# A gated scan and two feed-forward layers on one core: conversion of the weights on VectorE in pairs, the tanh ahead of the last block's cast, first tokens turned on TensorE

## The chip, the cores and the metric

The kernel runs on one core of one Trainium2 chip. The metric is the device time of an execution in microseconds (us); the time before is 2100.8 us, the median of three runs (2100.55 to 2101.74).

Engines are named as in the profile: PE is TensorE, DVE VectorE, ACT ScalarE, POOL GpSimd, SP the engine that issues most DMAs. Each executes its instructions in the order in which the program gives them, and waits where an operand isn't there yet.

## What is computed

```python
# x, f_logit: (2, 6080, 256)   weights: (256, 2048) and (2048, 256), 64-bit floats
f = lower_bound + (1 - lower_bound) / (1 + exp(-f_logit))
h = f[:, t] * h + (1 - f[:, t]) * x[:, t]      # for t in 6080 steps; y[:, t] = h
x = y.reshape(12160, 256)
h = x @ moe_w_in;   x = (h - tanh(h)) @ moe_w_out
h = x @ moe2_w_in;  return max(0.01 * h, h) @ moe2_w_out
```

The weights come as 64-bit floats, and the kernel reads them as pairs of 32-bit words. It multiplies with more precision than one product of TensorE's 32-bit format gives: each operand is split into a high half (rounded) and a low half (the rest), and three products are added up: high by high, high by low, low by high.

## The kernel before

The 12160 tokens are cut into macros of 1024 tokens. An item is one macro in one layer; items alternate between the layers. An item goes through 8 units of 256 hidden features. In the first three items (`NPLAIN`; layer 1, layer 1, layer 2) a unit is four **plain blocks** of 128 features by 512 tokens, 96 blocks in all; block s is the s-th. From the fourth item on a unit saves products with Strassen's scheme, in another loop.

A plain block is, in the loop over `order` at the end: `plain` (6 products into one of four PSUM banks, L381), `act` (the tanh, L391, or in layer 2 the leaky function, L393, on ACT), `shrink` (h - tanh(h), L399 on DVE, layer 1 only), then for its two halves `hi` (a rounding cast, L404 on ACT) and `lo` (the subtraction, L409 on DVE), and three blocks later `emit_B` (6 products with the output weights, L425). `rest` holds `hi` and `lo` of a block back until the products of the next one have been issued. `work(s)` runs what `put` has laid beside block s: conversion of weights, loads, the front end of the next macro and the splitting of its tokens (`make_forms`, `split_hi`, `split_lo`). All of it goes into the same engine queues, in the order of the code.

`convert` turns 256 columns of weights (one unit of w_in or w_out, 128 by 512 pairs of words) into high and low halves: L109, L115, L117, L127, L133 on DVE, L111, L121, L122 and the cast L135 on ACT, the addition L126 and the product L138 on POOL. The result goes to the tile that the unit uses (layer 1) or through a staging tile (layer 2), and to DRAM, from which later items stream it (`stream_a`, `stream_b`). Layer 1's units are converted during item 0, just ahead of their use, layer 2's during item 1. `sums_in` makes the four sums of blocks that Strassen's scheme needs, for a unit at a time.

The front end of a macro (`front`) turns f_logit and x so that features lie on the partitions: `load_tokens` reads runs of 32 features, and DVE transposes 32 by 32 blocks (L278). Then come the gate's tanh on ACT (L285), a scaling (L289), the input product (L296), and the scan in pieces of 256 tokens (L307).

Of the kernel before, what the change touches and what calls it, by code (L numbers as in the profile page):

```python
# [6 lines left out]

# [7 lines left out]
P = 128  # L15
# [4 lines left out]
def tile_gated_scan_two_ffn(  # L20
# [51 lines left out]

    lb = const.tile([P, KD], F32, name="lb")
# [19 lines left out]
    E_LO, E_HI = float(896 << 20), float(1151 << 20)  # L93

    def convert(load, halves, store):

        s = {}
        sh = [P, 2, 2 * P]

        def words(i, dt):  # L100
            return s["raw"].bitcast(dt).rearrange("p a (n t) -> p a n t", t=2)[:, :, :, i]

        def f0():
            s["raw"] = cv.tile(sh, U64, tag="raw", bufs=3, name="raw")
            nc.sync.dma_start(s["raw"], load)

        def s0():
            b = s["b"] = cv.tile(sh, I32, tag="b", bufs=2, name="b")
            nc.vector.tensor_scalar(b, words(1, I32), 0x7FFFFE00, None, op0=ALU.bitwise_and)  # L109
            s["l"] = cv.tile(sh, F32, tag="l", bufs=2, name="l")  # L110
            nc.scalar.activation(s["l"], words(0, U32), AF.Copy, scale=2.0**-52)  # L111

        def s1():
            b = s["b"]
            nc.vector.tensor_scalar(b, b, E_LO, E_HI, op0=ALU.max, op1=ALU.min)  # L115
            s["m"] = cv.tile(sh, I32, tag="m", bufs=2, name="m")
            nc.vector.tensor_scalar(s["m"], words(1, I32), 0x1FF, None, op0=ALU.bitwise_and)  # L117

        def s2():
            b = s["b"]  # L120
            nc.scalar.activation(b, b, AF.Copy, scale=8.0, bias=-8.0 * E_LO)  # L121
            nc.scalar.activation(s["m"].bitcast(F32), s["m"], AF.Copy, scale=2.0**-20)  # L122

        def s3():
            b = s["b"]
# [5 lines left out]
        def s4():  # L131
            s["e"] = cv.tile(sh, I32, tag="m", bufs=2, name="e")
            nc.vector.tensor_scalar(s["e"], s["b"], -(1 << 23), None, op0=ALU.bitwise_and)  # L133
            s["w"] = halves()
            nc.scalar.copy(s["w"][0], s["b"].bitcast(F32))  # L135

        def s5():
            nc.gpsimd.tensor_tensor(s["w"][1], s["l"], s["e"].bitcast(F32), ALU.mult)  # L138

        def s6():  # L140
            store()
            s.clear()

        return f0, [s0, s1, s2, s3, s4, s5, s6]

    def conv_in(l, u, dst):
# [13 lines left out]
        return convert(src, halves, store)  # L160

    def conv_out(l, u, dst):
# [10 lines left out]
        return convert(src, halves, store)  # L173

    def sums_in(l, u):

        s = {}
        sh = [P, 2, 2 * P]

        def v(i):  # L180
            return s["f"][:, i]

        def f0():
            s["raw"] = cv.tile(sh, U64, tag="raw", bufs=3, name="raw").bitcast(F32).rearrange(
                "p a (b q) -> p a b q", q=P
            )
            nc.sync.dma_start(s["raw"], wa_d[l][u][:, :, 0:4])

        def s0():
            s["f"] = cv.tile(sh, I32, tag="b", bufs=2, name="f").bitcast(F32).rearrange(  # L190
                "p k (f q) -> p (k f) q", q=P
            )
            nc.vector.tensor_tensor(s["f"], s["raw"][:, 0], s["raw"][:, 1], ALU.add)
            s["s"] = cv.tile(sh, F32, tag="l", bufs=2, name="s").rearrange(
                "p k (f q) -> p (k f) q", q=P
            )

        def s1():
            r = s["s"]
            nc.vector.tensor_tensor(r[:, 0], v(0), v(2), ALU.add)  # L200
            nc.vector.tensor_tensor(r[:, 2], v(1), v(0), ALU.subtract)

        def s2():
            r = s["s"]
            nc.vector.tensor_tensor(r[:, 1], r[:, 0], v(1), ALU.subtract)
            nc.vector.tensor_tensor(r[:, 3], v(3), r[:, 1], ALU.subtract)

        def s3():
            s["w"] = cv.tile([P, 2, 4, P], F32R, tag="sa", name="sa")
            nc.scalar.copy(s["w"][:, 0], s["s"])  # L210

        def s4():
            nc.vector.tensor_tensor(s["w"][:, 1], s["s"], s["w"][:, 0].bitcast(F32), ALU.subtract)

        def s5():
            nc.sync.dma_start(wa_d[l][u][:, :, 4:8], s["w"].bitcast(F32))
            s.clear()

        return f0, [s0, s1, s2, s3, s4, s5]
# [11 lines left out]

    def stage_a():
        return cv.tile([P, 2, 4, P], F32R, tag="sa", name="sa")

    def stage_b():
        return cv.tile([P, 2, 2, DM], F32R, tag="sb", name="sb")
# [18 lines left out]
    def load_tokens(c, k, nm, part=None, eng=None):  # L255

        t0, n = macros[c]
        a, e = part or (0, n)
        if (c, k, nm) not in raw:
            raw[c, k, nm] = fp.tile([P, 2 * H // 32, 32], F32, tag="raw", bufs=4, name=f"raw{nm}")  # L260
# [443 lines left out]
```

## Time and profile before

| | |
|---|---|
| median of three runs | 2100.8 us |
| the profiled execution | 2104.0 us |
| its span | 2102.2 us |
| TensorE busy | 2010.3 us, 96% of the span |
| VectorE busy | 1441.0 us, 69% |
| ScalarE busy | 1239.7 us, 59% |
| GpSimd busy | 85.8 us, 4%, all of it in the first 305 us |

The span is the part of the profiled execution between its first and last recorded instruction. Shares of the whole span hide stages: the plain blocks end at 380 us, a fifth of the way, and conversion lies within them. "Idle before" is the time for which an engine did nothing ahead of an instruction, with what released it. Where a row covers several instructions, its duration is that of all of them, from the first start to the last end; a start-to-start distance of two rows is what an instruction costs its engine in a dense stretch.

### The profile page before, as it was taken

What the parts mean: (1) busy time and instruction counts of PE and PEld (TensorE: products, weight loads), DVE (VectorE), ACT (ScalarE), POOL (GpSimd) and SP (SyncE); (2) the same over time, 40 slices, a digit from 0 to 9 for tenths busy, and PEclk for the clock granted to TensorE, in tenths of its full rate; (3) what the DMA queues carried; (4) which work ended last, traced back from release to release, by engine and by line L of the source; (5) the groups of instructions that cost most, each with busy time, mean ns of one, the idle gap of its engine ahead of it and who ended that gap; (6) DMA issues with size and microseconds to landing.
All of it is one profiled execution on the core that took longest, in us unless ns stands there. A gap on an engine that the chain in (4) does not pass through costs nothing.

```text
span 2102.2 us, 24666 instructions
## 1 busy us (share of the span) xinstructions
PE 2010.3 (96%) x8712; PEld 1651.7 (79%) x8712; DVE 1441.0 (69%) x2351; ACT 1239.7 (59%) x2272; POOL 85.8 (4%) x68
## 2 busy tenths in 40 slices
PE   3879889999999999999999999999999999999998
PEld 2656668777888888888888888888888888889887
DVE  6787767787677677677677677677667767666443
ACT  3546555565566566666666656556656656666654
POOL 2322320000000000000000000000000000000000
PEclk8979989999999999999999999999999999999999
DMA  5625586875555455446356356356356445454352
GB/s 140 170 96 180 195 231 197 267 223 172 169 167 159 141 172 162 151 167 183 139 157 178 143 164 190 142 158 178 138 162 189 151 158 166 144 176 148 146 177 83
DMA packets 399244, 348.32 MB, mean 166 GB/s; under 512 B 305936, under 2 KB 305936, under 8 KB 399120
## 3 DMA queue, kind: packets, MB, share of 16 engines
q1 hardware_dynamic: 394624, 346.22, 52.0%
q8 instruction: 69, 1.13, 0.2%
q10 hardware_dynamic: 4496, 0.53, 0.2%
q14 instruction: 55, 0.45, 0.1%
HBM read 309.07 MB, written 37.62 MB: 165 GB/s over the span
## 4 chain that ended last, share of the span: by engine, by line
PE 83%; DVE 7%; ACT 4%; DMA 2%; issue 2%; SPq 1%; POOL 0%; DVEq 0%; ACTq 0%; POOLq 0%
PE acc L425 44%; PE b L368 21%; PE c L368 16%; DVE g L399 2%; ACT gh L404 2%; DVE gl L409 1%; PE b L381 1%; PE c L381 1%; DMA raw<-in_moe_w_in_dram 1%; SPq L264 1%; ACT g L391 1%; DVE b L115 1%; ACT b L121 1%; ACT m L122 1%; DMA raw<-wa 0%
## 5 line engine op out<-in xcount | busy, mean ns | idle before, releaser
L425 PE MATMUL acc<-gh,wb 128*128 128x512 f32 (+1 forms) x3072 | 1050.7, 392 | 28.1 <-ACT gh L404 21.9
L425 PEld LDWEIGHTS acc<-gh,wb 128*128 128x128 f32 x3072 | 583.3, 190 | 152.5 <-ACT gh L404 29.9
L409 DVE TENSOR_TENSOR gl<-g,gh 128x512 fp32r<-128x512 f32 (+1 forms) x768 | 501.2, 680 | 278.8 <-ACT gh L404 270.8
L425 PE MATMUL acc<-gl,wb 128*128 128x512 f32 (+1 forms) x1536 | 604.2, 393 | 4.9 <-DVE gl L409 4.9
L404 ACT CAST gh<-g 128x512 fp32r<-128x512 f32 (+1 forms) x768 | 445.6, 616 | 186.5 <-DVE g L399 185.5
L368 PE MATMUL b<-xh,wa 128*128 128x512 f32 (+1 forms) x1344 | 493.0, 387 | 3.6 <-DVE c L644 3.6
L368 PE MATMUL c<-xh,wa 128*128 128x512 f32 (+1 forms) x1008 | 363.3, 387 | 0.2 <-DVE g L399 0.2
L425 PEld LDWEIGHTS acc<-gl,wb 128*128 128x128 f32 x1536 | 291.5, 190 | 73.1 <-DVE gl L409 16.2
L393 ACT ACTIVATE g<-c 128x512 f32<-128x512 f32 (+1 forms) x280 | 159.4, 602 | 249.3 <-PE c L368 231.7
L368 PEld LDWEIGHTS b<-xh,wa 128*128 128x128 f32 x1344 | 252.3, 188 | 54.2 <-DVE c L644 4.0
L368 PE MATMUL b<-xl,wa 128*128 128x512 f32 (+1 forms) x672 | 260.0, 387 | 0.0
L391 ACT ACTIVATE g<-c 128x512 f32<-128x512 f32 (+1 forms) x272 | 155.3, 600 | 168.5 <-PE c L368 161.2
L368 PEld LDWEIGHTS c<-xh,wa 128*128 128x128 f32 x1008 | 189.3, 188 | 38.2 <-DVE g L399 1.3
L399 DVE TENSOR_TENSOR g<-c,g 128x512 f32<-128x512 f32 (+1 forms) x272 | 177.6, 678 | 34.8 <-ACT g L391 32.2
L368 PE MATMUL c<-xl,wa 128*128 128x512 f32 (+1 forms) x504 | 195.2, 387 | 0.0
L664 DVE TENSOR_TENSOR c<-b,s 128x512 f32<-128x512 f32 (+1 forms) x168 | 115.0, 685 | 116.6 <-PE b L368 114.9
L610 ACT COPY c<-b 128x512 f32<-128x512 f32 (+1 forms) x168 | 94.9, 565 | 130.1 <-PE b L368 130.1
L644 DVE TENSOR_TENSOR c<-b,s 128x512 f32<-128x512 f32 (+1 forms) x168 | 116.1, 691 | 52.6 <-PE b L368 32.7
L368 PEld LDWEIGHTS b<-xl,wa 128*128 128x128 f32 x672 | 126.1, 188 | 24.6
L399 DVE TENSOR_TENSOR g<-b,g 128x512 f32<-128x512 f32 (+1 forms) x112 | 76.2, 680 | 92.8 <-ACT g L391 92.8
L633 ACT COPY s<-c 128x512 f32<-128x512 f32 (+1 forms) x168 | 98.1, 584 | 36.8 <-PE c L368 29.2
L368 PEld LDWEIGHTS c<-xl,wa 128*128 128x128 f32 x504 | 94.7, 188 | 18.5
(62 smaller groups left out, 1318.5 us busy)
## 6 DMA issues: line engine op xcount, KB each, us to landing
wa<-wa SPq DMA_DIRECT2D x168, 896.0 KB, 5.0
wb<-wb SPq DMA_DIRECT2D x192, 512.0 KB, 5.6
wa<-wa SPq DMA_DIRECT2D x24, 512.0 KB, 5.0
wa<-sa SPq DMA_DIRECT2D x24, 512.0 KB, 3.8
out_dram<-o SPq DMA_DIRECT2D x176, 64.0 KB, 1.9
rawf<-in_f_logit_dram SPq DMA_DIRECT2D x80, 128.0 KB, 5.5
rawx<-in_x_dram SPq DMA_DIRECT2D x80, 128.0 KB, 3.0
raw<-in_moe_w_in_dram SPq DMA_DIRECT2D x16, 512.0 KB, 5.0
```

Source lines behind the costliest of these rows:

```text
L368: nc.tensor.matmul(bank[:, :h], wt[:, s, w], xx[:, v, :h], start=start and i == 0, stop=i == 2, skip_group_check=True,)
L381: nc.tensor.matmul(bank[:, :h], wt[:, s, 2 * k + j], xx[:, v[k], :h], start=i == 0, stop=i == 5,)
L391: nc.scalar.activation(g[:, :h], src[:, :h], AF.Tanh)
L393: nc.scalar.activation(g[:, :h], src[:, :h], AF.Prelu, alpha=0.01)
L399: nc.vector.tensor_tensor(g[:, :h], u["src", name][:, :h], g[:, :h], ALU.subtract)
L404: nc.scalar.copy(gh[:, :h], u["g", name][:, :h])
L409: nc.vector.tensor_tensor(gl[:, :h], u["g", name][:, :h], u["hi", name][:, :h].bitcast(F32), ALU.subtract)
L425: nc.tensor.matmul(bank[e][:, :h], w[:, j, s, es], v[:, :h], start=first and i == 0, stop=i == 2, skip_group_check=True,)
L610: nc.scalar.copy(c11[:, :h], b1[:, :h])
L633: nc.scalar.copy(s5[:, :h], c12[:, :h])
L644: nc.vector.tensor_tensor(c12[:, :h], b1[:, :h], s5[:, :h], ALU.add)
L664: nc.vector.tensor_tensor(c22[:, :h], b1[:, :h], s5[:, :h], ALU.add)
```

## The change

It has four parts.

- **Conversion.** `convert` takes one or two units (`parts`): 1024 columns in one instruction for a unit of w_out and the next unit of w_in. ACT takes the absolute value (L116) and casts the high halves (L135); everything else is on DVE: a clamp in floating point (L120), shift and mask (L121), sign (L127), the mask of the low bits (L132), the sum of the low words (L138), the mask of the exponent (L143), and the product per unit (L149). L132, L138 and L143 write into the words of the raw tile. POOL has nothing of it. `raw` has two buffers instead of three, and layer 2's two units share one staging tile, `st`. Layer 2's pairs lie six blocks apart, from block 33 to block 81.
- **Sums.** `sums_in` takes two units at a time and begins at block 82 instead of 72.
- **Order within a block.** In the loop of plain blocks, `act` and `shrink` of block s come ahead of `rest` (cast and low half of block s-1) and of `work(s)`.
- **First macro.** `first_front` loads f_logit and x in whole rows, four DMAs in place of 32, turns them with 32 products by an identity matrix on PE into PSUM banks, and works from there.

```diff
             for v, j, n in order:
                 u, name, bank = us[v], f"c{2 - j}{n + 1}", hb[s % 4]
                 u["wa"] = wa[u["t"]]
                 plain(u, bank, name)
+                act(u, name, bank)
+                shrink(u, name)
                 if rest:
                     rest()
                 work(s)
-                act(u, name, bank)
-                shrink(u, name)
```

```diff
         def s1():
-            b = s["b"]
-            nc.vector.tensor_scalar(b, b, E_LO, E_HI, op0=ALU.max, op1=ALU.min)
-            s["m"] = cv.tile(sh, I32, tag="m", bufs=2, name="m")
-            nc.vector.tensor_scalar(s["m"], words(1, I32), 0x1FF, None, op0=ALU.bitwise_and)
+            b = s["b"].bitcast(I32)
+            nc.vector.tensor_scalar(s["b"], s["b"], W_LO, W_HI, op0=ALU.max, op1=ALU.min)
+            nc.vector.tensor_scalar(
+                b, b, 3, 0x3FFFF000, op0=ALU.logical_shift_left, op1=ALU.bitwise_and
+            )
...
         def s3():
-            b = s["b"]
-            nc.gpsimd.tensor_tensor(s["l"], s["l"], s["m"].bitcast(F32), ALU.add)
+            nc.vector.tensor_scalar(words(1, I32), words(1, I32), 0x1FF, None, op0=ALU.bitwise_and)
+            s["w"] = [halves() for _, halves, _ in parts]
+            for i, w in enumerate(s["w"]):
+                nc.scalar.copy(w[0], s["b"][:, 2 * i:2 * i + 2])
+
+        def s4():
             nc.vector.scalar_tensor_tensor(
-                b, words(1, I32), -(2**31), b, op0=ALU.bitwise_and, op1=ALU.bitwise_or
-            )
...
+                words(0, F32), words(0, U32), 2.0**-32, words(1, I32), op0=ALU.mult, op1=ALU.add
+            )
 
         def s5():
-            nc.gpsimd.tensor_tensor(s["w"][1], s["l"], s["e"].bitcast(F32), ALU.mult)
...
+            nc.vector.tensor_scalar(
+                words(1, I32), s["b"].bitcast(I32), -(1 << 23), None, op0=ALU.bitwise_and
+            )
+
+        def s6(i):
+            l, e = (words(j, F32)[:, 2 * i:2 * i + 2] for j in range(2))
+            nc.vector.scalar_tensor_tensor(
+                s["w"][i][1], l, 2.0**-20, e, op0=ALU.mult, op1=ALU.mult
+            )
+            parts[i][2]()
```

```diff
+        def turn(nm):
+            for k in range(KD):
+                for j in range(nb):
+                    nc.tensor.transpose(
+                        banks[nm][k][:, j * P:(j + 1) * P], s[nm][:, j, k * P:(k + 1) * P], ident
+                    )
...
         I = NS * NU
-        a, b = I + 2, 2 * I + 4
-        w = [f for u in range(NU) for f in (conv_in(1, u, stage_a), conv_out(1, u, stage_b))]
-        for i, (load, jobs) in enumerate(w):
-            p, q = (a + (b - a) * v // len(w) for v in (i, i + 2))
-            put(p - 1, [load])
-            put(p, jobs, q)
...
+        w = [convert([conv_in(1, u, stage_a), conv_out(1, u, stage_b)]) for u in range(NU)]
+        for u, (load, jobs) in enumerate(w):
+            put(I + 1 + 6 * u - 5, [load])
+            put(I + 1 + 6 * u, jobs, I + 7 + 6 * u)
```

VectorE before, two blocks in the middle of item 0 (g is a block's activation, gl its low half, b, e and m are tiles of the conversion; the numbers tell tiles apart):

```order
L399 TENSOR_TENSOR g_609<-b10_85,g_609 128x512
L409 TENSOR_TENSOR gl_626<-g_609,gh_624 128x512
L127 SCALAR_TENSOR_TENSOR b_598<-raw_515,b_598 128x512
L399 TENSOR_TENSOR g_637<-b11_86,g_637 128x512
L409 TENSOR_TENSOR gl_654<-g_637,gh_652 128x512
L133 TENSOR_SCALAR e_657<-b_598 128x512
L109 TENSOR_SCALAR b_662<-raw_571 128x512
L115 TENSOR_SCALAR b_662<-b_662 128x512
L117 TENSOR_SCALAR m_667<-raw_571 128x512
```

VectorE after, two blocks of the same item:

```order
L459 TENSOR_TENSOR g_524<-b10_86,g_524 128x512
L469 TENSOR_TENSOR gl_529<-g_500,gh_527 128x512
L120 TENSOR_SCALAR b_531<-b_531 128x1024
L121 TENSOR_SCALAR b_531<-b_531 128x1024
L127 SCALAR_TENSOR_TENSOR b_531<-raw_398,b_531 128x1024
L349 TENSOR_SCALAR tf_484<-tf_484,ga_83,gb_84 128x512
L459 TENSOR_TENSOR g_549<-b11_87,g_549 128x512
L469 TENSOR_TENSOR gl_554<-g_524,gh_552 128x512
L132 TENSOR_SCALAR raw_398<-raw_398 128x1024
L138 SCALAR_TENSOR_TENSOR raw_398<-raw_398 128x1024
L143 TENSOR_SCALAR raw_398<-b_531 128x1024
```

Before, the low half of a block (gl_626) follows the subtraction of that same block (g_609); after, the low half that follows a subtraction is the previous block's (gl_554 is of g_524, behind the subtraction of g_549). Conversion steps are twice as wide.

ScalarE before, at the same blocks as VectorE's first (gh is the cast):

```order
L391 ACTIVATE g_491<-b10_85 128x512
L404 CAST gh_506<-g_491 128x512
L121 ACTIVATE b_474<-b_474 128x512
L122 ACTIVATE m_479<-m_479 128x512
L391 ACTIVATE g_517<-b11_86 128x512
```

ScalarE after:

```order
L451 ACTIVATE g_549<-b11_87 128x512
L464 CAST gh_552<-g_524 128x512
L135 CAST wa_557<-b_531 128x512
L135 CAST wb_558<-b_531 128x2x256
L451 ACTIVATE g_578<-c11_88 128x512
```

A cast now stands behind the tanh of the next block and is of the block before it (gh_552 is of g_524, behind the tanh of g_549); the conversion's scalings L121 and L122 are gone from ScalarE.

## Rows read from the trace of the kernel before

**Rows 1.** Windows: stretch, length, busy PE, PEld, DVE, ACT, POOL, clock, DMA.

```profile
20.00:67.00 47.00, 32.91 (x112) 24.80 (x113) 37.29 (x63) 23.95 (x43) 13.35 (x10) 0.85 0.45 137
67.00:171.00 104.00, 83.44 (x279) 59.97 (x278) 81.27 (x127) 52.14 (x95) 26.54 (x20) 0.82 0.47 137
171.00:381.00 210.00, 188.48 (x749) 145.01 (x748) 148.67 (x258) 123.44 (x220) 42.97 (x32) 0.95 0.64 204
381.00:521.00 140.00, 134.09 (x575) 107.72 (x574) 112.95 (x205) 83.55 (x153) 0.00 (x0) 0.99 0.73 224
521.00:2102.00 1581.00, 1571.29 (x7004) 1314.07 (x7002) 1050.92 (x1682) 951.10 (x1754) 0.00 (x0) 1.00 0.49 158
```

**Rows 2.** The chain that ended last, in order of time: start, us, what.

```profile
333.00 1.36 PE acc L425 x6
334.36 1.36 PE c L381 x6
...
380.60 0.69 PE b L368 x3
```

**Rows 3.** Waits of VectorE from 20 to 290 us.

```profile
DVE gl L409 <- ACT gh L404: 43.2, 63, 0.7
DVE g L399 <- ACT g L391: 14.9, 26, 1.3
```

**Rows 4.** Timeline of VectorE: blocks 8, 31 and 32; start, us, instruction, idle before.

```profile
67.17 0.68 DVE L399 TENSOR_TENSOR g<-b,g 128x512 f32<-128x512 f32 x1
68.53 0.69 DVE L409 TENSOR_TENSOR gl<-g,gh 128x512 fp32r<-128x512 f32 x1 [0.69 <-ACT gh L404]
...
170.31 0.69 DVE L409 TENSOR_TENSOR gl<-g,gh 128x512 fp32r<-128x512 f32 x1 [0.69 <-ACT gh L404]
170.92 0.68 DVE L399 TENSOR_TENSOR g<-b,g 128x512 f32<-128x512 f32 x1
```

**Rows 5.** Timeline, VectorE and GpSimd: the clamp L115 twice; 51.70 is block 4.

```profile
51.02 0.43 DVE L115 TENSOR_SCALAR b<-b 128x512 int32<-128x512 int32 x1
51.36 0.42 DVE L117 TENSOR_SCALAR m<-raw 128x512 int32<-128x512 int32 x1
51.70 0.69 DVE L399 TENSOR_TENSOR g<-b,g 128x512 f32<-128x512 f32 x1
...
72.71 1.27 POOL L138 TENSOR_TENSOR wa<-l,e 128x512 fp32r<-128x512 f32 x1 [1.73 <-DVE e L133]
72.85 1.41 DVE L115 TENSOR_SCALAR b<-b 128x512 int32<-128x512 int32 x1
```

**Rows 6.** Groups of VectorE, 67 to 171 us: count, busy us, mean ns, idle.

```profile
L115 DVE TENSOR_SCALAR b<-b 128x512 int32<-128x512 int32 x9 | 12.8, 1424 | 0.3
...
L296 DVE SCALAR_TENSOR_TENSOR tx<-tf,tx 128x512 f32<-128x512 f32 x4 | 4.8, 1234 | 0.0
L307 DVE TENSOR_TENSOR_SCAN y<-tf,y,tx 128x256 f32<-128x256 f32 x6 | 4.5, 749 | 0.2
...
L289 DVE TENSOR_SCALAR tf<-tf,ga,gb 128x512 f32<-128x512 f32 x4 | 2.9, 776 | 0.0
...
L278 DVE STREAM_TRANSPOSE tf<-rawf 128x512 f32<-128x512 f32 x4 | 2.7, 694 | 0.0
```

**Rows 7.** Timeline of VectorE: two-tensor instructions of 128 columns.

```profile
317.71 0.29 DVE L200 TENSOR_TENSOR s<-f 128x128 f32<-128x128 f32 x1
317.92 0.28 DVE L201 TENSOR_TENSOR s<-f 128x128 f32<-128x128 f32 x1
```

**Rows 8.** Timeline of TensorE: the first product, and two products after a gap.

```profile
19.92 0.79 PE L381 MATMUL b<-xh,wa 128*128 128x512 f32 x1 [19.92 <-ACT xh L336]
...
109.76 1.22 PE L381 MATMUL b<-xh,wa 128*128 128x512 f32 x2 [4.05 <-ACT wa L135]
```

**Rows 9.** DMA issues: tile, count, KB each, median us from issue to landing.

```profile
wa<-sa SPq DMA_DIRECT2D x24, 512.0 KB, 3.8
```

More of the change, by code (lines that the diff above doesn't have):

```diff
@@ L107, in s0 @@
         def s0():
[L108 to L111, printed above, removed]
+            s["t"] = cv.tile(sh, F32, tag="c", bufs=2, name="b")
+            s["b"] = s["t"][:, :n]
+            nc.scalar.activation(s["b"], words(1, F32), AF.Abs)
         def s1():
-            b = s["b"]
@@ L146, in conv_in @@
+        return f0, [s0, s1, s2, s3, s4, s5] + [lambda i=i: s6(i) for i in range(len(parts))]
     def conv_in(l, u, dst):
@@ new lines, in f0, with blocks, s0, s1 @@
+            s["raw"] = raw
+            for i in range(2):
+                nc.sync.dma_start(raw[:, i], wa_d[l][u + i][:, :, 0:4])
+        def blocks(nm):
+            t = cv.tile(sh, F32, tag="c", bufs=2, name=nm)
+            return t.rearrange("p (n k) (f q) -> p n (k f) q", n=2, q=P)
+        def s0():
+            s["f"] = blocks("f")
+            nc.vector.tensor_tensor(s["f"], s["raw"][:, :, 0], s["raw"][:, :, 1], ALU.add)
+        def s1():
+            f, r = s["f"], blocks("s")
+            s["s"] = r
+            nc.vector.tensor_tensor(r[:, :, 0], f[:, :, 0], f[:, :, 2], ALU.add)
+            nc.vector.tensor_tensor(r[:, :, 2], f[:, :, 1], f[:, :, 0], ALU.subtract)
@@ L496, in tile_gated_scan_two_ffn @@
-        first_out[0][0]()
-        for nm in "fx":
-            for k in range(KD):
-                load_tokens(0, k, nm, halves[1])
-        first_in[1][0]()
+        to_a = [lambda u=u: wa_tile(u) for u in range(NU)]
+        to_b = [lambda u=u: wb_tile(u) for u in range(NU)]
+        first = [convert([conv_in(0, 0, to_a[0])])]
+        for u in range(NU):
+            nxt = [conv_in(0, u + 1, to_a[u + 1])] if u + 1 < NU else []
+            first.append(convert(nxt + [conv_out(0, u, to_b[u])]))
@@ L541, in tile_gated_scan_two_ffn @@
-        put(4 * I + 8, [lambda: conv.__exit__(None, None, None)])
+        run(front0[0:2] + first[0][1][0:2] + front0[2:4] + first[0][1][2:4] + front0[4:8])
+        run(mix(split0[0:4], first[0][1][4:]))
+        order0 = [(u, j, n) for n in range(2) for u in range(2) for j in range(2)]
+        put(0, first[1][1], 2)
+        put(0, [first[2][0]])
+        put(1, front1 + split0[4:8], 4)
+        put(3, first[2][1], 6)
+        for u in range(2, NU):
+            put(NS * u - 5, [first[u + 1][0]])
+            put(NS * u, first[u + 1][1], NS * u + 3)
@@ new lines, in tile_gated_scan_two_ffn @@
+        I = NS * NU
+        w = [convert([conv_in(1, u, stage_a), conv_out(1, u, stage_b)]) for u in range(NU)]
+        for u, (load, jobs) in enumerate(w):
+            put(I + 1 + 6 * u - 5, [load])
+            put(I + 1 + 6 * u, jobs, I + 7 + 6 * u)
+        a = 2 * I + 18
+        for l, at in ((0, (a, a + 5, a + 12, a + 20, a + 28)), (1, range(a + 28, a + 61, 8))):
+            for i in range(NU // 2):
+                load, jobs = sums_in(l, 2 * i)
+                put(at[i] - 5, [load])
+                put(at[i], jobs, at[i + 1])
```

175 lines of the change are left out of this document (85 added, 90 removed).

## Prediction, made before the changed kernel was run

> **What bounds the kernel now.** I read the busy time by stage first [rows 1]. From 381 us on TensorE is busy for 134.1 of 140 us and then for 1571.3 of 1581: nothing that VectorE is spared there can shorten anything. The loss lies ahead of it: 32.9 of 47 us, 83.4 of 104 (at a granted clock of 0.82), 188.5 of 210. The chain of work shows what these stages could take: in the last third of the plain blocks a block is two groups of six products, 1.36 us each, 2.72 us in all, and the plain blocks end at 380.6 us [rows 2]. There are 96 of them, 261 us, and the first product starts at 19.9 us [rows 8]. So some 100 us are lost in front.
>
> Who holds TensorE up: VectorE, which in the window of 104 us is busy for 81.3 us [rows 1] and waits for most of the rest. Its waits from 20 to 290 us are 43.2 us for the low half (L409) on ScalarE's cast of the same block, 63 times 0.7 us, and 14.9 us for the tanh [rows 3]. The timeline shows why [rows 4]: L399 of a block starts at 67.17, L409 only at 68.53 after 0.69 us of waiting, since the cast lies between two VectorE instructions that stand side by side. A second tax is GpSimd: the same clamp L115 takes 0.43 us alone and 1.41 us where a GpSimd product starts just before it [rows 5]; its mean in the 104 us is 1.42 us, and L296 (1.23) and L289 (0.78) are stretched too [rows 6].
>
> **Order within a block.** Now the tanh and the subtraction of block s precede the cast and low half of block s-1. The cast runs beside the subtraction, and its operand was made a block ago. The wait of 0.69 us goes for each of the 64 blocks with a tanh, 44 us of VectorE time. What is late next: the subtraction's wait for the tanh. The cast now queues on ScalarE behind a tanh that waits for TensorE, and TensorE needs that cast two blocks later. In a steady block the cast is ready about 3 us early (the product of block s+3 ends 3 x 2.72 after block s's; tanh, cast and low half of the next block take about 2.72 + 0.6 + 0.6 + 0.7 + 0.6), so it costs nothing while TensorE isn't starved.
>
> **Conversion.** VectorE starts its instructions 0.61 us apart for two-tensor forms of 512 columns (170.31 to 170.92) [rows 4] and 0.34 us apart for one-tensor forms (51.02 to 51.36) [rows 5]. At 128 columns the two-tensor step is 0.21 us [rows 7]. So 0.40 us buys 384 columns, the fixed part is 0.08, and 1024 columns take 1.14 us (two tensors) or half the slope, 0.61 us (one tensor). A pair of units then is 4 x 0.61 + 2 x 1.14 + 2 x 0.61 = 5.94 us, and about 0.5 us for five steps that depend on the one just before: 6.45 us. Before, a unit had three one-tensor steps, one two-tensor step and the clamp: 3 x 0.34 + 0.61 + 1.42 = 3.05 us and some 0.15 for steps that depend on the one before, a pair 6.4. VectorE gains nothing by itself here; GpSimd's two products per unit vanish, and with them the stretching elsewhere. Two of the one-tensor steps write every second word. No row shows such a write; a read of every second word goes at the one-tensor pace (L117) [rows 5]. If the write went at the two-tensor pace, a pair would cost 1.06 us more. I take the fast value, whose row is nearest, and keep the slow one as an end.
>
> The Trainium skill, "VectorE: DVE Perf Modes", section "What auto-detection actually checks", names one source, both operands in SBUF and an even outer dimension as the conditions of the double rate, and says nothing against a stride: by that, the fast value holds.
>
> **First tokens.** Eight VectorE turns leave, some 0.69 us each (L278) [rows 6], and 32 TensorE turns come. A turn of 128 columns lies between 0.06 us (a quarter of a product of 0.23) and 0.61 us (half of the 1.22 that two whole products take after a gap) [rows 8]. The first eight stand on the path, 0.5 to 5 us; I take 0.2 us each, the rest runs while VectorE works. Fewer, longer loads may give as much back, so I leave the first product at 20 us, between 17 and 25.
>
> The Trainium skill, "TensorE: Matmul & The Clock Gate", section "Part 4: PE-mode transpose", gives 275 to 390 ns for a turn of half this width in bytes: eight would be 2 to 3 us, an estimate that would put about 1 us on my sum.
>
> **The sum, by stages.** The marks are the starts of the subtraction.
> - To block 8. Before: 67.17 [rows 4]. After: block 0's subtraction at about 24, then up to block 4's, on VectorE: seven block instructions 4.3, a pair 6.45, scale and multiply of the second half of the first tokens 2.3, four scans and two copies 3.4, two low splits 1.2: 17.7, and 2.5 of waiting: 44 against 51.70 before [rows 5]. Then TensorE decides: 4 x 2.72, and 2 us for a low clock after its gap: 57. Bounds 54 to 66.
> - Blocks 8 to 32. Before: 170.92 - 67.17 = 103.8 [rows 4]. After, VectorE: 24 x 1.22 = 29.3; five pairs and one single unit 36; the next tokens' front end 19.3 from its groups [rows 6] (L278 and L307 have two groups each, of which the larger stands there) less 3.5 of stretching (four L296 and four L289, at the 0.69 and 0.43 us of their kinds [rows 4, 5]), 15.8; low splits 2.4. Together 84, against 65 of TensorE, so VectorE still leads. Waits come on top: the second weights of a unit are made in its third block and wanted by TensorE in the fourth; then a group of output products and one of input products must pass before the next tanh, 2 x 1.36 + 0.8 = 3.5 us, against 3.0 us of work that VectorE has left: 0.5 us a unit. At the low clock that a gap of 4 us leaves behind (two products 1.22 us) [rows 8] it is 6 against 3: 3 us a unit. Six units: 3 to 18 us; I take 10. So 94, bounds 87 to 108 with the slow write.
> - Block 32 to the end of the plain blocks. Before: 380.6 - 170.9 = 209.7. After: the second layer's conversion is spread to six blocks a pair, VectorE has 1.22 + 6.45/6 = 2.3 us a block against 2.72, and in blocks 64 to 81 the low half, conversion and front end 0.61 + 1.08 + 0.93 = 2.62. TensorE decides: 63 x 2.72 = 171, and 9 us for evacuations, the near-tie and clock: 180. Bounds 175 to 187.
> - After that: TensorE was 96% busy and better; the sums come later and in half the instructions. 0, give or take 3.
>
> Together 57 + 94 + 180 = 331 against 380.6: 50 us off a span of 2102.2, whose execution took 2104.0. The median of the runs is 2100.8, so 2051.
>
> **The rivals.**
> *Waits vanish* (0.12): no low clock, stage two at 87, start at 54, third stage 175: 65 us, 2036 and down to 2030. For it: fewer gaps on TensorE; against it: VectorE still has more work than TensorE up to block 32.
> *VectorE stays the bound for longer* (0.20): slow writes, 3 us a unit, a start at 66 and 187 at the end: 66 + 108 + 187 = 361, 20 us, 2081; the middle of this case is 2068.
> *The reordering only moves the wait* (0.04): ScalarE, in order, reaches the cast only after a tanh that is itself late, and L409 waits as before. Then the 44 us stay, and about 6 are left: 2095. Against it: in the timeline [rows 4] TensorE's products were ready each time; the 0.69 is the cast alone.
> *Slower* (0.03): the second layer's pairs and the sums share one staging tile. The cast into it waits for the last pair's stores, and ScalarE's next tanh queues behind that. There are 16 such casts; a store lands in 3.8 us [rows 9] and the cast comes three blocks, 8.2 us, after it. With 3 us of slack in the block loop, only landings of over 11 us cost anything; it takes 4 us more than that at each, 16 x 4 = 64, to give back 50 and end at 2115. Loads of tokens queued ahead on SP may delay one or two, not sixteen.
>
> **Chances.** The forecast has 0.61 (2038 to 2062). Of the case in which the wait only moves, half lies beyond 0.2%. The range takes in most of the two neighbours: 2030 to 2072. Faster by over 0.2%, about what a measurement of this kernel can tell from no change: 0.95; within: 0.02; slower: 0.03.
>
> **What would show it.** L459 and L469 side by side with no wait on the cast; L120 and L121 at 0.65 to 0.7 us for 1024 columns (1.2 for L132 and L143 would mean the slow write); the subtraction of block 8 near 57, of block 32 near 151; a block every 2.72 us from there; no change after 520 us. Wrong would make it: ScalarE casts waiting for a store, or TensorE gaps at every unit beyond block 32.

## The result and the profile after

The changed kernel takes 2048.5 us, the median of four runs (2048.2 to 2049.0), against 2100.9 us before (2100.55 to 2101.74; the 2100.8 above is the median without its fourth run): a ratio of 0.975, with a 95% interval from 0.9733 to 0.9767. The span of the profiled execution is 2046.6 us. The forecast was 2051.0.

The code after the change has other line numbers: L459 is the subtraction g - tanh (L399 before), L464 the cast and L469 the low half (L404 and L409), L451 the tanh, L441 the input products of the plain blocks, L485 the output products, L428 the products of the Strassen loop, L504 and L508 the turn and the store of outputs.

The windows of the changed kernel, cut at the starts of the subtraction of blocks 0, 8 and 32, near the end of the plain blocks, and 140 us after that; columns as in [rows 1]:

```profile
20.00:59.00 39.00, 27.42 (x82) 19.44 (x81) 28.58 (x43) 15.12 (x27) 0.00 (x0) 0.75 0.50 154
59.00:158.00 99.00, 76.99 (x289) 60.46 (x288) 82.00 (x125) 43.09 (x74) 0.00 (x0) 0.88 0.45 136
158.00:325.00 167.00, 166.55 (x733) 137.23 (x733) 139.45 (x209) 97.72 (x172) 0.00 (x0) 1.00 0.71 235
325.00:465.00 140.00, 139.31 (x613) 114.42 (x612) 118.26 (x191) 88.80 (x158) 0.00 (x0) 1.00 0.78 253
465.00:2046.00 1581.00, 1570.12 (x6995) 1312.20 (x6993) 1051.25 (x1682) 950.10 (x1752) 0.00 (x0) 1.00 0.49 158
```

From block 32 on TensorE has nothing left to gain: 166.55 of 167 us, at a granted clock of 1.00, where [rows 1] had 188.48 of 210 at 0.95. What is still lost lies ahead of it: 27 of 39 and 77 of 99 us. The chain that ended last shows the end of the plain blocks, at 331.35 in place of the 380.60 of [rows 2]:

```profile
328.63 1.36 PE c L441 x6
329.99 1.36 PE acc L485 x6
331.35 0.68 PE b L428 x3
```

The timeline of VectorE from block 8 on (start, us, instruction, in brackets the idle time before it):

```profile
59.11 0.69 DVE L459 TENSOR_TENSOR g<-b,g 128x512 f32<-128x512 f32 x1 [1.43 <-ACT g L451]
59.72 0.68 DVE L469 TENSOR_TENSOR gl<-g,gh 128x512 fp32r<-128x512 f32 x1
60.66 0.69 DVE L120 TENSOR_SCALAR b<-b 128x1024 f32<-128x1024 f32 x1 [0.26 <-ACT b L116]
61.39 0.69 DVE L121 TENSOR_SCALAR b<-b 128x1024 int32<-128x1024 int32 x1
62.12 1.23 DVE L127 SCALAR_TENSOR_TENSOR b<-raw,b 128x1024 int32<-128x1024 int32 x1
63.26 0.68 DVE L459 TENSOR_TENSOR g<-b,g 128x512 f32<-128x512 f32 x1
63.86 0.68 DVE L469 TENSOR_TENSOR gl<-g,gh 128x512 fp32r<-128x512 f32 x1
64.46 0.69 DVE L132 TENSOR_SCALAR raw<-raw 128x1024 int32<-128x1024 int32 x1
65.18 1.23 DVE L138 SCALAR_TENSOR_TENSOR raw<-raw 128x1024 f32<-128x1024 uint32 x1
66.44 0.70 DVE L143 TENSOR_SCALAR raw<-b 128x1024 int32<-128x1024 int32 x1
67.05 0.68 DVE L459 TENSOR_TENSOR g<-c,g 128x512 f32<-128x512 f32 x1
...
68.25 0.69 DVE L149 SCALAR_TENSOR_TENSOR wa<-raw 128x512 fp32r<-128x512 f32 x1
68.85 0.69 DVE L149 SCALAR_TENSOR_TENSOR wb<-raw 128x512 fp32r<-128x512 f32 x1
69.46 1.30 DVE L338 STREAM_TRANSPOSE tf<-rawf 128x512 f32<-128x512 f32 x2
...
74.46 0.69 DVE L459 TENSOR_TENSOR g<-b,g 128x512 f32<-128x512 f32 x1 [2.54 <-ACT g L451]
```

L459 and L469 stand side by side; the 0.69 us of [rows 4] is gone. The second weights, wb, are finished only at 69.5 us, and a new wait stands in its place once a unit: 2.54 us for the tanh at 74.46, the first block of the next unit. VectorE's waits in this stage, 59 to 158 us (us in total, times, longest):

```profile
DVE g L459 <- ACT g L451: 14.0, 6, 3.6
DVE b L120 <- ACT b L116: 1.3, 5, 0.3
```

The 14.0 us still hold block 8's own wait, 1.43, and not the one that ends at block 32, 2.19 (158.27). Between the two marks the tanh costs 14.8 us, at the first block of each of six units, and both rows together 16.1.

TensorE's waits over 0 to 340 us (the first of the seven lies ahead of block 8), then TensorE's timeline around one of them:

```profile
PE acc L485 <- DVE wb L149: 24.5, 7, 5.1
```

```profile
86.45 0.73 PE L485 MATMUL acc<-gh,wb 128*128 128x512 f32 x2 [4.06 <-DVE wb L149]
87.02 0.41 PE L485 MATMUL acc<-gl,wb 128*128 128x512 f32 x1
87.25 0.60 PE L485 MATMUL acc<-gh,wb 128*128 128x512 f32 x1
87.65 1.05 PE L441 MATMUL b<-xh,wa 128*128 128x512 f32 x2
88.50 1.05 PE L441 MATMUL b<-xl,wa 128*128 128x512 f32 x2
```

This is the circle: TensorE stands for 4.06 us for the second weights; soon after the gap its products come at 0.85 us a pair (87.65 to 88.50) in place of the 0.45 of a steady stretch (1.36 us for six), at a granted clock of 0.50 from 87.6 to 90.0 us, the lower of its two levels; the tanh behind them is late; VectorE waits for it, and starts the next conversion late.

### The profile page after: what moved, and what is told of

It reads as the page before. It is cut to its first block, busy times and chain, and to the rows that moved or that the text cites. A ratio compares the mean times of both kernels' runs of the same rounds, so it can differ in the third digit from the quotient of the medians.

```text
span 2046.6 us, 24457 instructions
## 1 busy us (share of the span) xinstructions
PE 1990.6 (97%) x8744; PEld 1652.0 (81%) x8744; DVE 1429.3 (70%) x2269; ACT 1199.8 (59%) x2185; POOL 0.7 (0%) x6
## 4 chain that ended last, share of the span: by engine, by line
PE 91%; DVE 5%; DMA 1%; ACT 1%; issue 1%; SPq 1%; DVEq 0%; ACTq 0%
PE acc L485 48%; PE b L428 22%; PE c L428 16%; PE b L441 3%; PE c L441 2%; DVE gl L469 1%; DVE g L459 1%; DVE raw L138 0%; SPq L508 0%; DMA out_dram<-o 0%; ACT b L116 0%; DMA wb<-st 0%; DVE b L127 0%; DMA wb<-wb 0%; ACT gh L464 0%
## 5 line engine op out<-in xcount | busy, mean ns | idle before, releaser
L485 PE MATMUL acc<-gh,wb 128*128 128x512 f32 (+1 forms) x3072 | 1043.9, 389 | 26.4 <-DVE wb L149 24.5
L485 PEld LDWEIGHTS acc<-gh,wb 128*128 128x128 f32 x3072 | 579.2, 189 | 146.0 <-DVE wb L149 27.3
L469 DVE TENSOR_TENSOR gl<-g,gh 128x512 fp32r<-128x512 f32 (+1 forms) x768 | 500.5, 679 | 222.5 <-ACT gh L464 214.3
L485 PE MATMUL acc<-gl,wb 128*128 128x512 f32 (+1 forms) x1536 | 597.2, 389 | 1.8 <-DVE gl L469 1.8
L464 ACT CAST gh<-g 128x512 fp32r<-128x512 f32 (+1 forms) x768 | 444.8, 615 | 86.7 <-DVE g L459 86.6
L428 PE MATMUL b<-xh,wa 128*128 128x512 f32 (+1 forms) x1344 | 492.6, 387 | 0.0
L428 PE MATMUL c<-xh,wa 128*128 128x512 f32 (+1 forms) x1008 | 362.6, 387 | 0.0
L485 PEld LDWEIGHTS acc<-gl,wb 128*128 128x128 f32 x1536 | 289.8, 189 | 61.2 <-DVE gl L469 3.8
L428 PEld LDWEIGHTS b<-xh,wa 128*128 128x128 f32 x1344 | 252.3, 188 | 49.2
L451 ACT ACTIVATE g<-c 128x512 f32<-128x512 f32 (+1 forms) x272 | 155.4, 602 | 209.8 <-PE c L428 168.2
L428 PE MATMUL b<-xl,wa 128*128 128x512 f32 (+1 forms) x672 | 260.0, 387 | 0.0
L428 PEld LDWEIGHTS c<-xh,wa 128*128 128x128 f32 x1008 | 189.2, 188 | 37.0
L459 DVE TENSOR_TENSOR g<-c,g 128x512 f32<-128x512 f32 (+1 forms) x272 | 177.7, 678 | 38.2 <-ACT g L451 35.3
L428 PE MATMUL c<-xl,wa 128*128 128x512 f32 (+1 forms) x504 | 195.0, 387 | 0.0
L661 ACT COPY c<-b 128x512 f32<-128x512 f32 (+1 forms) x168 | 94.9, 565 | 131.0 <-PE b L428 131.0
L459 DVE TENSOR_TENSOR g<-b,g 128x512 f32<-128x512 f32 (+1 forms) x112 | 76.4, 682 | 111.7 <-ACT g L451 111.5
L428 PEld LDWEIGHTS b<-xl,wa 128*128 128x128 f32 x672 | 126.1, 188 | 24.9
L428 PEld LDWEIGHTS c<-xl,wa 128*128 128x128 f32 x504 | 94.6, 188 | 18.6
```

Source lines behind the costliest of these rows:

```text
L428: nc.tensor.matmul(bank[:, :h], wt[:, s, w], xx[:, v, :h], start=start and i == 0, stop=i == 2, skip_group_check=True,)
L451: nc.scalar.activation(g[:, :h], src[:, :h], AF.Tanh)
L459: nc.vector.tensor_tensor(g[:, :h], u["src", name][:, :h], g[:, :h], ALU.subtract)
L464: nc.scalar.copy(gh[:, :h], u["g", name][:, :h])
L469: nc.vector.tensor_tensor(gl[:, :h], u["g", name][:, :h], u["hi", name][:, :h].bitcast(F32), ALU.subtract)
L485: nc.tensor.matmul(bank[e][:, :h], w[:, j, s, es], v[:, :h], start=first and i == 0, stop=i == 2, skip_group_check=True,)
```

## Experiments

Marks are the starts of the subtraction (L459, before L399) of blocks 0, 8 and 32 and the end of the plain blocks, in us, from the profiled execution of each kernel; "after" is the rest of the span. Medians are of all runs. The kernel before was run again beside each group of runs, with medians from 2100.6 to 2102.6 us, and the ratios are to those of the same group; its profiled execution, from which its marks come, took 2104.0 us, 3.1 over its median.

| kernel | block 0 | block 8 | 8 to 32 | 32 to end | end | after | median |
|---|---|---|---|---|---|---|---|
| before | 28.5 | 67.2 | 103.8 | 209.7 | 380.6 | 1721.6 | 2100.9 |
| changed | 20.5 | 59.1 | 99.2 | 173.1 | 331.4 | 1715.3 | 2048.5 |
| changed, old order | 22.7 | 61.8 | 101.7 | 186.9 | 350.5 | 1715.0 | 2068.0 |
| before, new order alone | 23.7 | 61.8 | 88.2 | 195.9 | 345.9 | 1721.8 | 2068.3 |
| before, new order and new start | 20.4 | 55.7 | 87.9 | 195.8 | 339.3 | 1724.5 | 2062.6 |
| changed, old start | 24.7 | 67.6 | 99.3 | 172.6 | 339.5 | 1714.1 | 2052.4 |
| changed, second weights first | 20.9 | 60.1 | 94.9 | 173.6 | 328.6 | 1715.5 | 2043.8 |
| changed, conversion two blocks earlier | 20.6 | 61.7 | 80.7 | 173.8 | 316.2 | 1715.8 | 2032.1 |
| both of these | 20.2 | 59.6 | 80.3 | 172.7 | 312.7 | 1715.6 | 2033.8 |
| both, and two steps more | 20.1 | 60.0 | 79.7 | 172.8 | 312.5 | 1715.1 | 2029.7 |
| two blocks earlier, old order | 22.8 | 61.9 | 96.3 | 185.3 | 343.6 | 1715.8 | 2061.1 |
| changed, last product on GpSimd | 20.8 | 59.7 | 97.2 | 172.4 | 329.3 | 1714.5 | 2044.8 |
| before, sums loaded earlier | 28.1 | 67.0 | 103.7 | 209.5 | 380.3 | 1721.6 | 2102.8 |
| before, sums later and loaded earlier | 28.7 | 67.6 | 103.8 | 208.9 | 380.2 | 1717.1 | 2099.1 |

### The parts: order, conversion, start

The changed kernel with the old order:

```diff
-                act(u, name, bank)
-                shrink(u, name)
                 if rest:
                     rest()
                 work(s)
+                act(u, name, bank)
+                shrink(u, name)
```

> The changed kernel with the old order within a block: cast and low half of block s-1 and the jobs beside the block stand ahead of the tanh and subtraction of block s again. Theory (the order takes a wait of 0.7 us off VectorE in each of 64 blocks): the low half waits for the cast again, some 64 times 0.69 us. To block 32 VectorE leads, so 32 x 0.69 = 22 us show there, less what the present waits at the end of each unit (17 us in six units) absorb; between blocks 32 and 64 VectorE is busy for 139 of 167 us, so 22 us more nearly fit. Time 2063 to 2090 us, against 2048.5. Rival (the order only moved the wait, and the gain is the conversion's): 2045 to 2052 us, and waits of VectorE of the same sum as with the change.

2068.0 us (ratio to before 0.9846, 0.9831 to 0.9861), 19.5 us over the changed kernel: the theory's range. The place was not the theory's: of the 19 us of span 2.7 lie ahead of block 8, 2.5 between blocks 8 and 32, 13.8 behind block 32. VectorE's waits from 59 to 158 us in this kernel show why:

```profile
DVE gl L469 <- ACT gh L464: 14.4, 21, 0.7
DVE b L120 <- ACT b L116: 1.8, 5, 0.4
DVE g L459 <- ACT g L451: 1.5, 3, 0.8
```

Cut at this kernel's own blocks 8 and 32 (61.8 and 163.6 us), the cast costs 15.8 us, 23 times, where the changed kernel has 14.8 for the tanh. Between blocks 8 and 32, then, the order did little more than move the wait, as the rival had it. Behind block 32 it removed it: there VectorE waits for the cast 47 times, 35.2 us, with the old order and 15 times, 14.4 us, in the changed kernel, all of these past the last subtraction, at 243.0, and beside a TensorE that is busy for 85.6 of 86 us (245 to 331).

The other way round, the kernel before with the new order alone (the same lines, + and - exchanged):

> The kernel before with the new order within a block and nothing else. Theory (the order is the largest part): the 63 waits of 0.69 us for the cast go; 17 to 22 us come off the way to block 32, and blocks 32 to 96 fall from 210 us to between 176 and 190, as TensorE's 2.72 us a block decides there: 2052 to 2070 us. Rival (conversion with GpSimd holds VectorE up as much): the stretched instructions stay and the waits for the tanh take the place of those for the cast: 2078 to 2092 us. Second rival (the order only moves the wait): 2097 to 2103 us.

2068.3 us (0.9848, 0.9833 to 0.9863). 32.3 us against before in the same group, 62% of the whole gain, come from two moved lines. Here blocks 8 to 32 fall to 88.2 us, 11 us less than in the changed kernel, though GpSimd still stretches VectorE: the old conversion begins a unit's second weights two blocks ahead of the unit, the new one in its first block.

The kernel before with the new order and the new start, so that against the changed kernel conversion and sums alone are old:

```diff
-        for a, b in zip(f00, f01):
-            a[0](), b[0]()
-            if first_in[0][1]:
-                first_in[0][1].pop(0)()
+        turn0("f"), turn0("x"), turn1("f"), turn1("x")
+        run(front0[0:2] + first_in[0][1][0:2] + front0[2:4] + first_in[0][1][2:4] + front0[4:8])
```

> The kernel before with the new order within a block and the first tokens turned on TensorE, but with the old conversion (single units, two products on GpSimd) and the old sums. Theory (conversion costs VectorE the same per pair of units, 6.4 us, either way; what it brings is the end of the stretching, some 10 us of VectorE time, and the sums' earlier loads, 4 to 6 us): 2054 to 2066 us, so within 20 us of the changed kernel. Rival (the conversion is the larger half of the gain): 2072 us or more.

2062.6 us (0.9823, 0.9809 to 0.9838), in the theory's range, and for other reasons. Conversion and sums are worth 14 us as medians, but that is a difference of large terms: from this kernel to the changed one block 8 comes 3.5 us later, blocks 8 to 32 take 11.3 us more, block 32 to the end takes 22.7 us less, and the rest 9.2 us less. The gain behind block 32 goes with the second layer's conversion; what of it is the wider spacing (six blocks a pair in place of four), what the earlier loads of raw weights (five blocks ahead in place of one) and what GpSimd's absence was not taken apart. The loads may have a part: in this kernel VectorE waits for them between block 32 and the end, in the changed kernel it does not (total, times, longest).

```profile
DVE b L111 <- DMA raw<-in_moe_w_in_dram: 7.8, 6, 4.2
```

GpSimd's part looks small, at least with the wider spacing: with one of its two steps put back (a version below), the changed kernel takes 172.4 us from block 32 to the end, no longer than without. Of the 9.2 us in the rest, some 3 may be this kernel's profiled execution, 3.0 us over its median.

The changed kernel with the old start:

```diff
-        load0("f", nc.sync)
-        load0("x", nc.scalar)
+        load_tokens(0, 0, "f", halves[0])
+        load_tokens(0, 0, "x", halves[0], nc.scalar)
```

> The changed kernel with the old start: first tokens read in runs of 32 features by 32 DMAs and turned by VectorE. Theory (the turn on TensorE brought the first product from 19.9 to 16.4 us and took four turns, 2.8 us, off VectorE between blocks 0 and 4, where VectorE leads): 2051 to 2057 us, 3 to 8 us over the changed kernel. Rival (blocks 0 to 8 wait for the converted weights and not for tokens, and TensorE's low clock at the start gives the rest back): 2047 to 2050 us.

2052.4 us (0.9768, 0.9752 to 0.9785; runs from 2050.2 to 2055.4): 4 us by the medians. In the profiled execution, the slowest of the four, block 8 comes 8.5 us later. The theory's range holds. (The changed kernel's first product is at 15.5 us; the 16.4 of the theory is its second.)

### The late second weights

The changed kernel with the last two products of a conversion exchanged:

```diff
-        return f0, [s0, s1, s2, s3, s4, s5] + [lambda i=i: s6(i) for i in range(len(parts))]
+        return f0, [s0, s1, s2, s3, s4, s5] + [lambda i=i: s6(i) for i in reversed(range(len(parts)))]
```

> The changed kernel with the two last products of a conversion in the other order: the second weights of a unit, which TensorE wants first, 0.69 us ahead of the first weights of the next. Theory (gaps for the second weights): each of seven gaps shortens by 0.7 us and leaves less low clock behind, 5 to 9 us in all: 2039 to 2044 us. Rival (VectorE's work sets the pace): 2046 to 2050 us.

2043.8 us (0.9722, 0.9708 to 0.9735). 0.6 us a unit earlier saved 4.3 us between blocks 8 and 32, six units. Then the conversion begun two blocks earlier:

```diff
-            put(NS * u - 5, [first[u + 1][0]])
-            put(NS * u, first[u + 1][1], NS * u + 3)
+            put(NS * u - 6, [first[u + 1][0]])
+            put(NS * u - 2, first[u + 1][1], NS * u + 1)
```

> The changed kernel with the conversion of layer 1's units 2 to 7 begun two blocks earlier (at blocks 6 to 8 of every 8 in place of 8 to 10, and its loads one block earlier). Theory (between blocks 8 and 32 TensorE stands still once a unit, 24.5 us in seven gaps, for the second weights, which are ready a block too late, and VectorE then waits for tanhs): the gaps go, VectorE works through at 82 to 85 us, so blocks 8 to 32 take 84 to 90 us in place of 99: 2034 to 2041 us against 2048.5. Rival (VectorE's work sets the pace, the gaps are only where it shows): blocks 8 to 32 stay over 95 us, 2044 to 2050 us.

2032.1 us (0.9664, 0.9648 to 0.968), 16 us under the changed kernel and a little below the theory's range. The window of blocks 8 to 32, then TensorE's waits from 0 to 340 us:

```profile
60.00:142.00 82.00, 69.87 (x285) 54.39 (x284) 77.85 (x121) 39.92 (x70) 0.00 (x0) 0.96 0.56 159
```

```profile
PE acc L485 <- DVE gl L469: 12.1, 9, 2.8
...
PE acc L485 <- DVE wb L149: 3.4, 1, 3.4
```

VectorE now works for 77.85 of 82 us (some 5 us have moved ahead of block 8, which comes 2.6 us later), and TensorE's granted clock is 0.96 in place of 0.88. Of the seven waits for second weights one is left, ahead of block 8. Block 32 comes 15.9 us earlier, and VectorE's work up to it is the same, 119.5 us against 120.3: it was the gaps that cost these 16 us.

Both edits together:

> Both: conversion of units 2 to 7 two blocks earlier and the second weights first. Theory: past block 8 the earlier start already takes the gaps away and the order of the two products adds nothing there; ahead of block 8, where the pair for units 1 and 2 is not moved, the gap of 3.3 us at 48.8 us shortens, 0.7 to 2 us: 2033 to 2040 us, 0 to 2 us under the earlier start alone. Rival (VectorE's work sets the pace): 2044 to 2050 us.

2033.8 us (0.9669, 0.9655 to 0.9682), not to be told from the earlier start alone, as the theory said for the stretch past block 8; the 0.7 to 2 us ahead of it don't show in the medians (in the profiled executions block 8 comes 2 us earlier).

And with the two waits that were still to be seen ahead of block 32 (the loads of the later pairs, too, go out one block earlier here):

```diff
-        put(3, first[2][1], 6)
+        put(2, first[2][1], 5)
-            put(NS * u - 6, [first[u + 1][0]])
+            put(max(NS * u - 7, 1), [first[u + 1][0]])
-                at = ((8, 14) if it == 0 else (base - 4, base + 2))
+                at = ((5, 11) if it == 0 else (base - 4, base + 2))
```

> The changed kernel with the conversion of units 2 to 7 two blocks earlier and the second weights first, and now also the pair for units 1 and 2 one block earlier and the second macro's tokens loaded from block 5 in place of 8. Theory (what is left ahead of block 32 are single waits: 2.5 us of TensorE for the second weights near 48 us, 2.15 us of VectorE for tokens near 71 us): 2 to 5 us under the version without these two: 2027 to 2032 us. Rival (VectorE, busy for 77 of 82 us there, takes up both): 2031 to 2035 us.

2029.7 us (0.9655, 0.964 to 0.967; 2028.7 to 2031.1), the fastest kernel here, 19 us under the changed one. Against the two before it the runs overlap, so the last two steps are worth between nothing and 4 us.

The last of this group goes back to the order. If the late weights had absorbed it between blocks 8 and 32, then it must show there once they are gone:

> The version with the conversion of units 2 to 7 begun two blocks earlier, with the old order within a block. What is open: undoing the order in the changed kernel itself cost only 2.5 us between blocks 8 and 32, where 24 waits of 0.69 us, 16.6 us, were expected. Theory (there the waits at the end of each unit, which come from the late second weights, absorbed it): without those waits the 16.6 us show: blocks 8 to 32 take 93 to 98 us in place of 80.7, and 12 to 15 us more come after block 32 as in the changed kernel; 2056 to 2064 us against 2032. Rival (the order is worth little while VectorE leads): blocks 8 to 32 under 88 us, 2045 to 2052 us.

2061.1 us (0.9811, 0.9795 to 0.9828). Blocks 8 to 32 take 96.3 us in place of 80.7, 15.6 more, where the changed kernel showed 2.5, and the order is worth 29 us here in place of 19.5. VectorE's waits from 61 to 158 us in this kernel:

```profile
DVE gl L469 <- ACT gh L464: 16.5, 24, 0.7
```

24 waits, one a block, 16.5 us, and 15.6 of them show in the stage. Behind block 32 11.5 us more come, a little under the theory's 12 to 15.

### GpSimd

The changed kernel with the last product on GpSimd (without its factor):

```diff
-            nc.vector.scalar_tensor_tensor(
-                s["w"][i][1], l, 2.0**-20, e, op0=ALU.mult, op1=ALU.mult
-            )
+            nc.gpsimd.tensor_tensor(s["w"][i][1], l, e, ALU.mult)
```

> The changed kernel with the last product of the conversion (the low halves, 16 instructions of 512 columns) on GpSimd as before the change; the factor of 2 to the -20 in it is left out, so the low halves have the wrong size. Theory (GpSimd's products hold up VectorE instructions that run beside them, and take longer themselves, 1.27 us against 0.69): VectorE instructions that begin beside them stretch by up to 1 us each, which uses up the 16 x 0.69 = 11 us that VectorE is spared, and the second weights come 1 to 2 us later, so the gaps of TensorE grow: 2049 to 2060 us. Rival (GpSimd's work costs VectorE nothing here): VectorE is spared 0.69 us twice a unit while it leads, 2040 to 2046 us.

2044.8 us (0.9727, 0.9713 to 0.974; 2043.8 to 2046.5): 3.7 us faster than the changed kernel by the medians. The runs don't overlap, but the intervals of the two ratios to before just do (0.9733 to 0.974), so the size is uncertain. My theory, a loss of 0.5 to 11.5 us, fell. TensorE's seven gaps for the second weights, which it had grow, are 20.8 us in place of 24.5. GpSimd, then VectorE, at the same time:

```profile
84.00 1.04 POOL L149 TENSOR_TENSOR wa<-raw 128x512 fp32r<-128x512 f32 x1 [13.49 <-DVE raw L143]
85.00 1.04 POOL L149 TENSOR_TENSOR wb<-raw 128x512 fp32r<-128x512 f32 x1
```

```profile
84.05 0.70 DVE L336 STREAM_TRANSPOSE tx<-rawx 128x512 f32<-128x512 f32 x1
84.68 0.65 DVE L457 TENSOR_TENSOR g<-c,g 128x512 f32<-128x512 f32 x1
85.25 1.33 DVE L467 TENSOR_TENSOR gl<-g,gh 128x512 fp32r<-128x512 f32 x1
```

The stretching is there: the low half (L467 in this kernel) began 0.25 us after GpSimd's second product and took 1.33 us in place of 0.68. But the transpose and the subtraction beside the first product took their usual 0.70 and 0.65. From 59 to 158 us the low half's mean is 768 ns, against 679 in the changed kernel, over 25 of them, and that of the split L398 894 against 685 over four: 3.1 us paid for eleven products, which cost VectorE 0.60 us each, 6.6 us. It comes out ahead.

### The 6 us behind the plain blocks

In the kernel before the chain stood still once behind the plain blocks (start, us, what): a load for a sum of blocks, and VectorE waiting for it.

```profile
464.44 9.58 DMA raw<-wa
474.04 0.70 DVE f L193
```

The load five blocks ahead in place of three:

```diff
-                put(p - 3, [load])
+                put(p - 5, [load])
```

> The kernel before with the loads for the sums of blocks issued five blocks ahead of their use in place of three, and nothing else. Theory (the 6.3 us that the changed kernel gains behind the plain blocks are the stall of VectorE at 464 to 474 us, where a sum waits for its load): the stall goes, 2094 to 2097 us against 2100.6. Rival (the gain there comes from fewer instructions, or the stall is made up later): 2099 to 2102 us.

2102.8 us, no difference (1.0003, 0.9994 to 1.0011). The waits of TensorE from 381 to 521 us, of the kernel before and then of this one:

```profile
PE b L368 <- DVE c L644: 3.6, 1, 3.6
PE acc L425 <- DVE o L444: 1.5, 1, 1.5
PE acc L425 <- DVE gl L409: 0.6, 2, 0.4
```

```profile
PE acc L425 <- DVE o L444: 3.5, 1, 3.5
PE acc L425 <- DVE gl L409: 0.6, 2, 0.4
```

The 3.6 us behind the load are gone, and the wait for an output's turn, L444, which stood at 1.5, is 3.5. Then the sums at the changed kernel's places as well, still a unit at a time:

```diff
-        for l, a, b in ((0, 2 * I + 8, 3 * I + 4), (1, 3 * I + 4, 4 * I + 6)):
+        a = 2 * I + 18
+        for l, at in ((0, (a, a + 5, a + 12, a + 20, a + 28)), (1, range(a + 28, a + 61, 8))):
...
-                put(p - 3, [load])
+                put(p - 5, [load])
```

> The kernel before with its sums of blocks at the places where the changed kernel has them: from block 82 in place of 72, loads five blocks ahead in place of three, still a unit at a time. What is to be told apart: whether the 6 us that the changed kernel gains behind the plain blocks come from the place of the sums or from their being half as many instructions. Theory A (place and lead): the stalls of TensorE between 380 and 480 us, 5.5 us in the kernel before, go: 2093 to 2098 us against some 2101. Theory B (number of instructions and loads, which queue on SP and VectorE among the stores of the outputs): the stalls stay or move: 2099 to 2104 us.

2099.1 us (0.9987, 0.9978 to 0.9996), so 1 to 5 us are won: 1 us above theory A's range and at the lower edge of theory B's. In its profile TensorE is busy for 137.0 of the 140 us behind the plain blocks, against 134.1 before and 139.3 in the changed kernel. The place and lead of the sums, together, give some half of it or more; that the remaining 2 us are the halved number of instructions is no more than argued.

## Why the forecast held, and which of its steps did not

**The sum held by offsets.** It put the end of the plain blocks at 331 us; it came at 331.35. By terms, against the forecast: block 8 at 59.1 in place of 57, blocks 8 to 32 99.2 in place of 94, block 32 to the end 173.1 in place of 180, and behind that 6.3 us less where 0 to 3 was the bound. +2.1, +5.2, -6.9, -6.3: the first three cancel, and that the sum came so near is in part luck. By the spans the gain is 55.6 us, by the medians 52.4 against the forecast 50: the profiled execution of before was 3.1 us slower than the median, and in which of the stages these 3.1 us lie isn't shown.

**The order.** Its mechanism was right for the kernel as a whole: the waits of 0.69 us for the cast, 63 of them [rows 3, 4], are gone, and the order is the largest single part (32 us alone). What I did not see is that between blocks 8 and 32 the wait that goes and the new waits, which the sum has as terms of their own, are one thing: while the weights come late, VectorE waits for the cast or for the tanh, some 15 us either way. The rival in which reordering only moves the wait, at 0.04, was true of this stage, through late weights and not through ScalarE's queue.

**The late second weights.** The step named the place rightly (made in the unit's third block, wanted in the fourth) and left 3 to 18 us for it. VectorE's busy time was 82.0 against the forecast 84; the waits between the marks 16.1, against 10: that is the mis-sized term. A unit's first block waited 1.6 to 3.6 us for its tanh, where I had 0.5 without a low clock and 3 with it: 2.5 on the mean of six, two of them over 3. Ahead of block 8 I had left the same wait out: TensorE waited 3.3 us for unit 1's second weights and VectorE 4.6 us for the tanh behind it, hence 16.7 us from block 4 (42.4) to block 8 where the sum had 4 x 2.72 + 2 = 13.

**Block 32 to the end.** TensorE does decide there, as forecast: 173.1 us, of which 171 are its products. The 9 us that I put on top for evacuations, the near-tie in blocks 64 to 81 and the clock were the mis-sized term: 2.1, below my lower bound of 175.

**Conversion.** A pair of units costs VectorE 6.40 us by the distances of starts in the timeline above (0.73, 0.73, 1.14, 0.72, 1.26, 0.61, and twice 0.60), against 6.45. The open question of the strided write is answered by the groups of the changed kernel from 0 to 340 us (count, busy us, mean ns, idle):

```profile
L143 DVE TENSOR_SCALAR raw<-b 128x1024 int32<-128x1024 int32 x15 | 10.4, 696 | 0.5
L121 DVE TENSOR_SCALAR b<-b 128x1024 int32<-128x1024 int32 x15 | 10.4, 695 | 0.5
...
L132 DVE TENSOR_SCALAR raw<-raw 128x1024 int32<-128x1024 int32 x15 | 10.3, 688 | 0.0
```

L132 and L143 write every second word and take what L121 takes: the fast value. The Trainium skill, "VectorE: DVE Perf Modes", section "What auto-detection actually checks", names no stride among the conditions of the double rate for 32-bit words, and these rows agree with it. The end of the stretching, which I credited with 3.5 us, was real: the four multiplies went from 1234 to 684 ns and the four scalings from 776 to 541, 3.1 us. But "nothing on GpSimd" is not a gain in itself: with one product left there, without its factor, the kernel was 3.7 us faster by the medians, a size that is uncertain.

**The start.** Eight turns take 1.94 us, 0.24 each, near the 0.2 that I took; TensorE's timeline at the start:

```profile
5.70 1.94 PE L296 MATMUL b<-ident,rawf 128*128 128x128 f32 x8 [5.70 <-DMA rawf<-in_f_logit_dram]
...
15.50 0.52 PE L441 MATMUL b<-xh,wa 128*128 128x512 f32 x1
```

The first product came at 15.5 us, not 20 and not within 17 to 25; with the old loads and VectorE's turns it is at 18.9 in the otherwise changed kernel. By the traces the fewer, longer loads gave back more than the turns cost: the first f_logit is turned from 5.7 us on, where in the old start VectorE waits 4.8 us for the second half of it and turns that at 10.7. Loads and turns were only undone together, so this is read from the traces and not tested apart. The Trainium skill, "TensorE: Matmul & The Clock Gate", section "Part 4: PE-mode transpose", gives 275 to 390 ns for a single turn of half this width in bytes; the trace has 243 ns for each of eight in a row at the full width, and the measurement decides.

**The slower rival** did not come. ScalarE's waits for the shared staging tile, from 150 to 400 us, are this row:

```profile
ACT st L135 <- DMA wb<-st: 2.4, 2, 1.5
```

**Behind the plain blocks** I had read TensorE as 96% busy and better and put 0. The 134.1 of 140 us in [rows 1] became 139.3: 5.2 of the 6.3 us lay in that row, and I called it full.

## What to carry to other kernels

A wait that is taken away in a stage is worth something there only if no other wait of that stage grows into its place: the order of two lines was worth 2.5 us between blocks 8 and 32 beside late weights, and 15.6 us without them. When two steps are merged into one wider step, look up when each half is wanted: the pair had the same cost as two single units, but made the more urgent half two blocks later, and giving these blocks back was worth 16 us. A stall that is cut at one place (the load of the sums) can come back at the next (2.0 of 3.6 us in the output's turn, and no difference in the time), so an edit is priced by the end of the stage, not by the row that vanishes.

## What the runs showed of the hardware

GpSimd's hold on VectorE depends on the VectorE instruction. Beside GpSimd products of 1.04 us, a two-tensor instruction with both operands in SBUF took 1.33 us in place of 0.68, and it ended at 86.58 us, 0.54 after GpSimd's end at 86.04; a transpose (0.70) and a subtraction that reads one operand from PSUM (0.65) beside the same pair of products lost nothing. The other rows of these traces fit: of the instructions that started inside a GpSimd product in the plain blocks of the kernel with one product on GpSimd, 17 low halves took 1.14 us on the mean, 14 such subtractions 0.65 to 0.69 and four transposes 0.67 to 0.70. In the kernel before, the clamp with one operand took 1.38 to 1.45 us each of the 21 times that it started inside one, against 0.43 [rows 5]. The Trainium skill, "SBUF — State Buffer", section "🔬 SBUF: two separate sides", describes a port pair that is locked for a whole instruction, on VectorE's side by fast-mode instructions and by those with two inputs in SBUF; these rows agree with it. So in these kernels an instruction moved to GpSimd is cheap where the VectorE instructions behind it are transposes or read PSUM, and dear where they are not.
